# DeltaNet scan with an MLP-mixer on one core: the channel product in 15 block products, joins of units in pairs, a shorter weight rounding, norms on ScalarE, and a new written order

## The chip, the cores and the metric

One core of one Trainium2 chip runs the whole program. The metric is the device time of one launch in microseconds (us). The kernel before was timed three times: 692.44 us median (691.64 to 694.02).

## The reference

There are two stages. The first is a linear-attention scan ("DeltaNet") over 4 elements of 8 heads, 768 tokens and 48 features. For each token `t`, with `k_n = k / (|k| + 1e-6)`:

```
y[t]   = q[t] @ state
v_old  = k_n[t] @ state
state += beta[t] * outer(k_n[t], v[t] - v_old)
```

The second takes `x`, which is `y` as 4 x 768 tokens x 384 channels, and applies two small networks, first over tokens and then over channels:

```
h   = relu(x^T @ w_tok1) @ w_tok2          # 768 -> 256 -> 768 tokens
u   = x + h^T
out = u + relu(u @ w_ch1) @ w_ch2          # 384 -> 1536 -> 384 channels
```

Weights arrive as float64 and are rounded to float32 on the chip.

## The kernel before, in words

**The scan.** Each element's tokens are cut into 6 units of 128 tokens, 24 units in all, and each unit into two steps of 64 tokens, 48 steps. For each unit `prep(u)` (job `p`) squares and sums the keys, forms the norms (L396 to L403), transposes keys and queries on TensorE (L412, L428), multiplies them (L443) and masks the products on VectorE (L450). The masked 64x64 triangles need an inverse. `invert(rnd)` (job `i`) inverts their 32x32 diagonal blocks for a round of up to four units together, in a long series of pairs of VectorE operations (L561, L566). `join(u)` (job `j`) then fills the off-diagonal 32x32 block with two small products: `p_z` (L627), which ScalarE copies to `zst` (L630), and `p_x` (L636), copied into place (L639). Units 0 to 5 are inverted in 16x16 blocks first, with a smaller join, `join_16` (job `h`, L596 to L612), half of whose copies run on VectorE (`EARLY_DVE`). `recur(t)` (job `r`) takes one step of the scan: `p_k` (L660), `rest` on VectorE (L664), `p_y` and `p_w` (L677, L681), a ScalarE copy (L685), `p_s` and `p_y` (L693, L694), the new state on VectorE (L703), and the output rows on ScalarE (L708).

**The weights.** 34 pieces (jobs `w`) come by DMA as 64-bit words. `round_weights` takes each through six operations: on ScalarE a scaling of the low words (L256) and a square of the high words (L268), on GpSimd an add (L269), and on VectorE a shift (L257), an insertion of the sign (L262), and a compare-and-multiply (L271) that sets values of tiny magnitude to zero.

**The mixer.** `mixer(b)` (job `m`) is one element's second stage: the token products (L818, L831), then the channel products for three pairs of 128-token chunks. For element 0 the first channel product is plain: 12 tiles of hidden channels x 3 blocks of 128 input channels over 256 tokens (L904). For elements 1 to 3 `wide_fast` does it with sums of blocks: of the 12 block products that 2 x 3 blocks on 2 chunks need it makes 11, in two groups of three tiles each, so 66 products of 128x128 by 128x128 for each pair (L749). TensorE runs each product as two instructions here, so 132. The results are collected in `r2` by ScalarE copies (L776 to L795), VectorE adds (L766) and ScalarE relus (L769). The sums of weight blocks come from `sum_weights` (job `s`, L727); the sums of token blocks are four VectorE operations in `turn_pair` (L869). The second channel product has seven block products of 12 instructions each (L923) into two accumulators, `p_o` and `p_o2`. VectorE makes the operands `s1`, `s2` and `a21` (`halves_of`, L885) and adds the accumulators to `xb` (L849).

**The order.** Nothing is scheduled automatically. Every job is a generator, and a long string, `order`, lists which job takes its next step. Each engine executes its own instructions in the order in which that string issues them. `x`, `z`, `Y` are products of zeros on TensorE (L205, L215), whose results nobody reads. The last word is `m3*114`: the last 114 steps of element 3's mixer stand alone.

PSUM tiles of the mixer come from a pool of three banks (`ps_mlp`); a bank's next product waits until its last reader is done.

Of the kernel before, what the change touches and what calls it, by code (L numbers as in the profile page):

```python
# [13 lines left out]
C = 64  # L14
# [9 lines left out]
def kernel(  # L24
# [82 lines left out]
    EARLY_DVE = (1, 3)  # L107
# [6 lines left out]
    nc.scalar.sqrt(warm[0:1, 128:129], warm[0:1, 128:129])  # L114
    ident = const.tile([128, 128], FP32, name="ident")
# [65 lines left out]
    wcs = lent[:, 0 : 3 * NM * 128].rearrange("p (i m n) -> p i m n", i=3, m=NM)  # L181
# [60 lines left out]
    def round_weights(dst, src, name):  # L242

        n = dst.shape[-1]
        d64 = loads.tile([128, WP], mybir.dt.int64, name="d64", bufs=3)[:, 0:n]  # L250
        nc.sync.dma_start(out=d64, in_=src)
        yield
        words = d64.bitcast(U32).rearrange("p (n two) -> p n two", two=2)
        lo, hi = words[:, :, 0], words[:, :, 1]
        f = mlp_pool.tile([128, WP], U32, name="w_f", tag="r1")[:, 0:n]
        nc.scalar.activation(lo, lo, ACTF.Copy, scale=2.0**-29)  # L256
# [5 lines left out]
        nc.vector.scalar_tensor_tensor(  # L262
            out=f, in0=hi, scalar=0xC0000000, in1=f,
            op0=ALU.bitwise_and, op1=ALU.bitwise_or,
        )
        yield
        a = hi.bitcast(FP32)
        nc.scalar.square(a, a)  # L268
# [111 lines left out]
    def prep(u):  # L380
# [15 lines left out]
        nc.scalar.sqrt(nrm_f, ksum)  # L396
        yield
        nc.vector.tensor_scalar_add(nrm_f, nrm_f, 1e-6)
        cs = work.tile([128, NP, 2], FP32, name="cs")
        rec = work.tile([128, NB], FP32, name="rec")  # L400
        nc.vector.reciprocal(rec, nrm_f)
        nc.vector.tensor_tensor(out=rec, in0=rec, in1=rec, op=ALU.mult)
        nc.vector.tensor_tensor(  # L403
            out=cs, in0=rec.rearrange("s (p c) -> s p c", c=2), in1=bet, op=ALU.mult
# [180 lines left out]
    def join_16(u):  # L585
# [24 lines left out]
        for i, (block, _, _) in enumerate(quarters(u)):  # L610
            on = nc.vector.tensor_copy if i in EARLY_DVE else nc.scalar.copy
            on(out=block[0:QB, :, QB:HB], in_=p_x[HB * i : HB * i + QB])  # L612
            joined_16.add((u, i))
            yield

    def join(u):
# [3 lines left out]
        halves = [(slice(r.start, r.start + HB), slice(r.start + HB, r.stop)) for r in PAR]  # L620
        assert done.issuperset([(u, 0), (u, 2)])
        nc.vector.transpose(t11, wt[:, :, 0:HB])
        yield
        p_z = ps_prep([128, NB, HB], "p_z")
        for nb in range(NB):
            for r, r2 in halves:
                nc.tensor.matmul(p_z[r2, nb], wt[r, nb, HB:C], t11[r, nb])  # L627
        yield
        for r, r2 in halves:
            nc.scalar.copy(zst[r2], p_z[r2])  # L630
        yield
        assert done.issuperset([(u, 1), (u, 3)])
# [5 lines left out]
        for r, r2 in halves:  # L638
            nc.scalar.copy(wt[r, :, HB:C], p_x[r])  # L639
# [73 lines left out]

    def sum_weights():
        a = wc1.rearrange("p cb (m k n) -> p cb m k n", m=NM, k=2)
        for cb in range(2):
            for f in range(NHT):
                piece_of(wc1, cb, f * 128)
        a11, a21, a12, a22 = a[:, 0, :, 0], a[:, 0, :, 1], a[:, 1, :, 0], a[:, 1, :, 1]
        s1, s2, s4 = (wcs[:, i] for i in range(3))  # L720
        for i, (out, x, y, op) in enumerate((
            (s1, a21, a22, ALU.add), (s2, s1, a11, ALU.subtract),
            (s4, a12, s2, ALU.subtract), (a21, a11, a21, ALU.subtract),
        )):
            if i == 3:
                assert FAST in starts
            nc.vector.tensor_tensor(out=out, in0=x, in1=y, op=op)  # L727
            summed.add(i)
            yield

    starts = set()

    def wide_fast(u_t, t, r2):
        own = u_t[:, :, 0:U], u_t[:, :, U : 2 * U]
        b11, b21, b22 = own[0][:, 0], own[0][:, 1], own[1][:, 1]
        t1, t2, t4, t3 = t[:, 0], t[:, 1], t[:, 2], own[1][:, 0]
        def w(m, cb, k):
            f = (2 * m + k) * 128
            return wc1[:, cb, f : f + 128]

        lo, hi = slice(0, U), slice(U, 2 * U)
        n = NM // 2

        def bank(name):
            return ps_mlp([128, n, U], name)

        def product(p, weight, b_, first=False):
            for i in range(n):
                nc.tensor.matmul(  # L749
                    p[:, i], weight(g * n + i), b_, start=first and i == 0, stop=True,  # L750
                    skip_group_check=True,
                )

        def plain(cb, k):
            return lambda m: w(m, cb, k)

        def mixed(i):
            assert i in summed
            return lambda m: wcs[:, i, m]

        for g in range(2):
            ms = slice(g * n, g * n + n)
            c11, c12, c21, c22 = (r2[:, ms, k, e] for k in range(2) for e in (lo, hi))

            def add(out, p):
                nc.vector.tensor_tensor(out=out, in0=p, in1=out, op=ALU.add)  # L766

            def relu(out):
                nc.scalar.activation(out, out, ACTF.Relu)  # L769

            p_r = bank("p_r")
            product(p_r, plain(1, 0), b21, True)
            yield
            p_x = bank("p_c")
            product(p_x, plain(0, 0), b11, True)
            nc.scalar.copy(c11, p_x)  # L776
            yield
            product(p_r, plain(2, 0), own[0][:, 2])
            add(c11, p_r)
            yield  # L780
            p_y = bank("p_d")
            product(p_y, mixed(0), t1, True)
            nc.scalar.copy(c22, p_y)
            yield
            product(p_x, mixed(1), t2)
            nc.scalar.copy(c12, p_x)
            yield
            p_r = bank("p_r")
            product(p_r, plain(1, 1), t4, True)
            product(p_r, plain(2, 1), own[0][:, 2])  # L790
            relu(c11)
            yield
            assert 3 in summed
            product(p_x, plain(0, 1), t3)
            nc.scalar.copy(c21, p_x)  # L795
            yield
            product(p_y, mixed(2), b22)
            product(p_y, plain(2, 0), own[1][:, 2])
            add(c21, p_r)
            add(c12, p_y)  # L800
            yield
            product(p_x, plain(2, 1), own[1][:, 2])
            relu(c21)
            relu(c12)
            add(c22, p_x)
            yield
            relu(c22)
            yield
            yield g * n + n - 1

    def mixer(b):
# [42 lines left out]
        def turn_pair(c):  # L854
# [6 lines left out]
            t = mlp_pool.tile([128, 3, U], FP32, name="t_c", tag="r1")  # L861
            b11, b21, b12, b22 = (
# [239 lines left out]
```

## Time and profile before

| | |
|---|---|
| Median of three runs | 692.44 us (691.64 to 694.02) |
| The profiled execution's own time | 692.83 us |
| Its span in the profile | 691.0 us |
| Mean granted TensorE clock | 0.936 |
| Read from HBM, written to HBM | 35.49 MB, 9.44 MB |

The span runs from the first to the last instruction of the profiled execution; 1.8 us of its time lie around it. In the profile PE is TensorE's matmuls, PEld its weight loads (which run ahead beside matmuls), DVE is VectorE, ACT ScalarE, POOL GpSimd and SP the queue that issues DMAs. Line numbers are those of the kernel before. In a list of groups the columns are: line, engine, operation, out<-in, shape, xcount | busy us, mean ns of one | idle time ahead, and what ended it. In a timeline they are: start us, length us, engine, line, operation, xcount [idle ahead <- what ended it].

### The profile page before, as it was taken

Reading aid. Unit: us, or ns where it says so; the run is one execution under the profiler, and the core shown is the slowest. Engines: PE = TensorE matmul, PEld = TensorE weight load, DVE = VectorE, ACT = ScalarE, POOL = GpSimd, SP = SyncE. Lnnn points to the kernel's source line nnn. Section 1 sums busy time; section 2 is a strip of 40 time slices with the busy share of each in tenths; the row PEclk is TensorE's granted clock in tenths of the full one; section 3 lists DMA queues with packets and bytes.
Section 4 is the critical chain, followed back from the end, with each engine's and each line's share of the span. In section 5 each row is a group of like instructions: output and inputs, shape, how many; then the busy total and the mean of one; then the engine's idle time right before and its main releaser. Section 6 shows DMA issues by size and latency. Waiting matters only on the chain.

```text
span 691.0 us, 22497 instructions
## 1 busy us (share of the span) xinstructions
PE 643.6 (93%) x9696; PEld 562.2 (81%) x9696; DVE 428.9 (62%) x1135; ACT 272.7 (39%) x659; POOL 103.1 (15%) x121
## 2 busy tenths in 40 slices
PE   7548977689999999999999999999999999999998
PEld 5336766557899998877999999868989996999997
DVE  6988677887888853696464985347823332252433
ACT  7647666334732243213642514234425051132230
POOL 1345245213420112010120100100000000000000
PEclk9757677579999999999999999999999999999999
DMA  9744565545453334322444004020020000000000
GB/s 183 153 102 108 116 147 119 148 119 124 91 107 83 78 67 82 84 49 65 70 75 98 15 24 84 28 54 9 17 63 2 16 10 0 24 1 24 1 24 24
DMA packets 146915, 46.39 MB, mean 67 GB/s; under 512 B 138080, under 2 KB 141280, under 8 KB 146816
## 3 DMA queue, kind: packets, MB, share of 16 engines
q1 hardware_dynamic: 146816, 44.95, 29.8%
q8 instruction: 76, 1.25, 0.8%
q14 instruction: 23, 0.19, 0.1%
HBM read 35.49 MB, written 9.44 MB: 65 GB/s over the span
## 4 chain that ended last, share of the span: by engine, by line
PE 81%; DVE 7%; DMA 3%; SPq 3%; ACT 3%; issue 2%; POOL 0%; DVEq 0%; ACTq 0%; POOLq 0%
PE p_o L923 24%; PE p_r L749 8%; PE p_c L749 7%; PE p_d L749 5%; PE p_c L904 5%; PE p_h L831 5%; PE p L818 4%; PE p_k L660 4%; PE p_y L677 3%; PE p_g L443 3%; PE p_s L693 3%; PE p_z L627 2%; DVE sub L561 2%; PE p_warm L205 2%; PE p_x L636 2%
## 5 line engine op out<-in xcount | busy, mean ns | idle before, releaser
L923 PE MATMUL p_o<-wc,r 128*128 128x192 f32 x720 | 126.4, 329 | 0.6 <-ACT u_t L845 0.6
L923 PEld LDWEIGHTS p_o<-wc,r 128*128 128x128 f32 x720 | 116.6, 190 | 2.4 <-ACT u_t L845 1.1
L849 DVE TENSOR_TENSOR xb<-xb,p_o 128x192 f32<-128x192 f32 x84 | 29.5, 352 | 69.9 <-PE p_o L923 69.4
L561 DVE TENSOR_TENSOR sub<-x 128x84 f32<-128x84 f32 (+24 forms) x178 | 60.4, 339 | 8.1 <-DMA x<-n_dram 4.4
L566 DVE TENSOR_TENSOR x<-x,sub 128x84 f32<-128x84 f32 (+24 forms) x178 | 60.1, 338 | 6.1
L766 DVE TENSOR_TENSOR r<-p_r,r 128x384 f32<-128x384 f32 x36 | 20.0, 555 | 53.5 <-ACT r L795 42.2
L364 POOL TENSOR_TENSOR v_st<-v_st,nrm 128x384 f32<-128x384 f32 x24 | 20.6, 860 | 211.9 <-DMA v_st<-in_v_dram 187.0
L923 PE MATMUL p_o<-wc,s 128*128 128x192 f32 x288 | 50.7, 329 | 0.7 <-DVE xb L849 0.7
L904 PE MATMUL p_c<-u_t,wc 128*128 128x256 f32 x216 | 50.3, 385 | 0.0
L708 ACT ACTIVATE xb<-p_y 64x192 f32<-64x192 f32 x96 | 31.2, 325 | 47.0 <-PE p_y L694 20.4
L269 POOL TENSOR_TENSOR w_f<-w_f,d 128x384 uint32<-128x384 uint32 (+1 forms) x34 | 34.0, 1007 | 98.7 <-DVE w_f L262 49.8
L923 PEld LDWEIGHTS p_o<-wc,s 128*128 128x128 f32 x288 | 46.8, 190 | 1.3 <-DVE xb L849 1.0
L749 PE MATMUL p_r<-u_t,wc 128*128 128x128 f32 x324 | 46.5, 280 | 0.0
L749 PE MATMUL p_c<-u_t,wc 128*128 128x128 f32 x324 | 45.3, 276 | 0.0
L904 PEld LDWEIGHTS p_c<-u_t,wc 128*128 128x128 f32 x216 | 39.9, 190 | 5.6 <-issue 0.2
L769 ACT ACTIVATE r<-r 128x384 f32<-128x384 f32 x72 | 37.5, 523 | 17.2 <-DVE r L766 15.1
L685 ACT COPY w_t<-p_w 128x192 f32<-128x192 f32 x48 | 15.3, 319 | 67.8 <-PE p_w L681 67.3
L749 PEld LDWEIGHTS p_r<-u_t,wc 128*128 128x128 f32 x324 | 41.4, 194 | 0.4
L749 PEld LDWEIGHTS p_c<-u_t,wc 128*128 128x128 f32 x324 | 40.5, 192 | 0.2
L450 DVE TENSOR_TENSOR gm<-p_g,mb 128x512 f32<-128x512 f32 x44 | 28.8, 682 | 15.7 <-PE p_g L443 14.8
L776 ACT COPY r<-p_c 128x384 f32<-128x384 f32 x18 | 8.6, 479 | 73.9 <-PE p_c L749 67.8
L818 PE MATMUL p<-xb,w 128*128 128x384 f32 x96 | 36.4, 529 | 0.0
(170 smaller groups left out, 1284.9 us busy)
## 6 DMA issues: line engine op xcount, KB each, us to landing
d<-in_moe_w_ch_dram SPq DMA_DIRECT2D x24, 384.0 KB, 3.8
v_st<-in_v_dram SPq DMA_DIRECT2D x96, 48.0 KB, 2.7
out_dram<-xb SPq DMA_DIRECT2D x23, 192.0 KB, 1.9
kpad<-in_k_dram SPq DMA_DIRECT2D x18, 192.0 KB, 3.9
qpad<-in_q_dram SPq DMA_DIRECT2D x18, 192.0 KB, 3.6
kst<-in_k_dram SPq DMA_DIRECT2D x64, 48.0 KB, 2.8
n_dram<-gm SPq DMA_DIRECT2D x72, 32.0 KB, 2.5
gm<-w_dram SPq DMA_DIRECT2D x72, 32.0 KB, 2.1
```

Source lines behind the costliest of these rows:

```text
L269: nc.gpsimd.tensor_tensor(out=f, in0=f, in1=lo, op=ALU.add)
L450: nc.vector.tensor_tensor(out=blocks(gm)[:, :, cc, D:GW].rearrange("s p (two n) -> s p two n", two=2), in0=p_g[cc], in1=mb[:, :, cc, None, ...
L561: nc.vector.tensor_tensor(out=tmp, in0=y[:, :, 0:s, s : s + 1].to_broadcast([n, k, s, w]), in1=y[:, :, s : s + 1, s + 1 : m].to_broadcast( ...
L566: nc.vector.tensor_tensor(out=y[:, :, 0:s, s + 1 : m], in0=y[:, :, 0:s, s + 1 : m], in1=tmp, op=ALU.add,)
L708: nc.scalar.mul(y[:, :, D * i : D * i + D], p_y[PAR[1 - i]], 1.0 if c else -1.0)
L749: nc.tensor.matmul(p[:, i], weight(g * n + i), b_, start=first and i == 0, stop=True, skip_group_check=True,)
L769: nc.scalar.activation(out, out, ACTF.Relu)
L818: nc.tensor.matmul(p_1[dh], piece_of(w1, c, 0)[:, dh * 128 : (dh + 1) * 128], xb[:, c], start=(c == 0), stop=(c == NCH - 1),)
L831: nc.tensor.matmul(p_h, piece_of(w2, j, c * 128)[:, c * 128 : (c + 1) * 128], r1[j], start=(j == 0), stop=(j == NDH - 1),)
L849: nc.vector.tensor_tensor(out=xb[:, c, e], in0=xb[:, c, e], in1=p, op=ALU.add)
L904: nc.tensor.matmul(p_c[:, k], piece_of(wc1, cb, f * 128)[:, f * 128 : (f + 1) * 128], u_t[:, cb], start=(cb == 0), stop=(cb == NCB - 1),)
L923: nc.tensor.matmul(p, a[:, m], wc2[:, m, j], start=(start and m == 0), stop=(m == NM - 1), skip_group_check=True,)
```

## The change

1. **First channel product, elements 1 to 3.** The 1536 hidden channels are taken as 3 blocks of four tiles, and the 18 block products (3 x 3 blocks on 2 chunks) are made from 15 products of sums. Each has four matmuls, so 60 for a pair of chunks, 120 instructions. The 15 follow each other in four chains, each of which accumulates in one bank; after each product the bank is read into one block of `r2`, once into two. `sum_weights` grows from 4 operations of 768 elements to 17 of 512 or 256, 10 of them written over blocks of the weights, after the plain product of element 0 has used the block. The sums of token blocks (`forms`) grow from 4 to 11 operations. `halves_of` runs after all 15 products, in two parts, and the second channel product takes its tiles in the order 2 to 5, 0, 1.
2. **Joins.** In rounds from unit 6 on, the `p_x` products of a unit are issued between the `p_z` products of the next unit of its round, one for one; the last unit's follow alone.
3. **Rounding.** The compare-and-multiply that sets tiny values to zero is gone; the high word is scaled by 2^-112 on ScalarE instead of squared, and two VectorE operations do what three did.
4. **Norms.** The added 1e-6 and the square move from VectorE to ScalarE.
5. `EARLY_DVE` is gone: the 12 small copies it put on VectorE run on ScalarE.
6. **A new order** string. It ends in `m3*153`. It calls the products of zeros at other places: 8 instead of 11 of the 512-wide, 3 instead of 7 of the 128-wide, 20 instead of 12 of the small ones.

The core of the diff:

```
-        nc.scalar.activation(lo, lo, ACTF.Copy, scale=2.0**-29)
+        a = hi.bitcast(FP32)
+        nc.scalar.activation(a, a, ACTF.Copy, scale=2.0**-112)
+        nc.scalar.activation(lo, lo, ACTF.Copy, scale=2.0**-29)
+        yield
         nc.vector.tensor_scalar(
-            out=f, in0=hi, scalar1=0x07FFFFFF, scalar2=3,
+            out=f, in0=hi, scalar1=0x0FFFFFFF, scalar2=3,
...
-        nc.vector.scalar_tensor_tensor(
-            out=f, in0=hi, scalar=0xC0000000, in1=f,
...
-        nc.scalar.square(a, a)
         nc.gpsimd.tensor_tensor(out=f, in0=f, in1=lo, op=ALU.add)
         yield
         nc.vector.scalar_tensor_tensor(
-            out=dst, in0=a, scalar=(1.125 * 2.0**-15) ** 2, in1=f.bitcast(FP32),
-            op0=ALU.is_ge, op1=ALU.mult,
+            out=dst.bitcast(U32), in0=hi, scalar=0x80000000, in1=f,
+            op0=ALU.bitwise_and, op1=ALU.bitwise_or,
...
         nc.scalar.sqrt(nrm_f, ksum)
-        nc.vector.tensor_scalar_add(nrm_f, nrm_f, 1e-6)
-        nc.vector.reciprocal(rec, nrm_f)
-        nc.vector.tensor_tensor(out=rec, in0=rec, in1=rec, op=ALU.mult)
+        nc.scalar.activation(nrm_f, nrm_f, ACTF.Identity, bias=eps)
+        nc.scalar.square(ksum, nrm_f)
+        nc.vector.reciprocal(ksum, ksum)
...
         for nb in range(NB):
             for r, r2 in halves:
                 nc.tensor.matmul(p_z[r2, nb], wt[r, nb, HB:C], t11[r, nb])
+                if before:
+                    w = gm_of(before)[:, :, TC]
+                    nc.tensor.matmul(p_x[r, nb], zst[r2, nb], w[r2, nb, HB:C])
...
+        for n, (out, x, y, op) in enumerate((
+            ("u5", b[0, 0], b[2, 1], add), ("u12", b[1, 0], b[2, 0], add),
+            ("u3", b[0, 1], b[1, 1], add), ("u2", "u3", b[0, 0], sub),
+            ("u6", b[0, 1], b[0, 0], sub), ("u13", "u12", b[2, 1], sub),
+            ("u7", b[0, 1], b[2, 1], add), ("u4", b[1, 0], "u2", sub),
+            ("u8", "u13", b[1, 1], sub), ("u10", b[0, 0], b[2, 0], add),
+            ("u15", b[2, 0], b[2, 1], sub),
+        )):
...
+        for chain, n, reads in (
+            (1, 1, ((0, 0, 1, 0),)), (4, 12, ((0, 0, -1, 0),)), (2, 5, ((2, 0, 1, 0),)),
+            (1, 2, ((0, 1, 1, 0),)), (4, 13, ((0, 1, -1, 0),)), (2, 6, ((2, 1, 1, 0),)),
+            (1, 3, ((1, 1, 1, 0),)), (4, 14, ((2, 1, 1, 0),)), (1, 4, ((1, 0, 1, 0),)),
+            (2, 7, ((1, 1, 1, 1),)), (3, 10, ((1, 0, 1, 1), (2, 0, -1, 0))),
+            (2, 8, ((2, 1, -1, 1),)), (4, 15, ((2, 0, 1, 1),)), (3, 11, ((0, 0, 1, 1),)),
+            (2, 9, ((0, 1, 1, 1),)),
+        ):
...
+            for i in range(FT):
+                at = i % width * 128
+                nc.tensor.matmul(
+                    p[:, i], pieces[i // width][:, at : at + 128], f[f"u{n}"],
+                    start=first and i == 0, stop=True, skip_group_check=True,
+                )
+            yield
+            for j, e, sign, last in reads:
+                o = part(j, e)
+                if (j, e) not in begun:
+                    nc.scalar.copy(o, p)
+                    begun.add((j, e))
+                else:
+                    nc.vector.tensor_tensor(
+                        out=o, in0=o, in1=p, op=ALU.add if sign > 0 else ALU.subtract
+                    )
+                if last:
+                    nc.scalar.activation(o, o, ACTF.Relu)
+            yield
+        yield slice(2, NM)
+        yield slice(0, 2)
```

More of the change, by code (lines that the diff above doesn't have):

```diff
@@ L623, in join, with into @@
         yield
+        def into(x, w):
+            for r, r2 in halves:
+                nc.scalar.copy(w[r, :, HB:C], x[r])
+        assert len(left_over) == (not first)
+        before = None if first else left_over.pop()
+        assert first or done.issuperset([(before, 1), (before, 3)])
         p_z = ps_prep([128, NB, HB], "p_z")
+        p_x = ps_prep([128, NB, HB], "p_x") if before else None
         for nb in range(NB):
@@ L630, in join @@
             nc.scalar.copy(zst[r2], p_z[r2])
+        if before:
+            into(p_x, gm_of(before)[:, :, TC])
+            joined.add(before)
+        if not last:
+            left_over.append(u)
         yield
+        if not last:
+            return
         assert done.issuperset([(u, 1), (u, 3)])
@@ L731 @@
[L731 to L772, printed above, removed]
-            yield
[L774 to L809, printed above, removed]
@@ L893, in mixer @@
             if b >= FAST:
[L894 to L896 removed]
+                for ms in wide_fast(t_c, r2):
+                    if ms is not None:
+                        halves_of(ms)
                     yield
```

292 lines of the change are left out of this document (173 added, 119 removed).

## The prediction

> **What bounds the kernel now.** I read the page first, then its stretches, and cut them where step 11 of the scan, element 0's last, begins; from there the mixer can run.
>
> ```profile
> span 691.0 us, 22497 instructions
> PE 643.6 (93%) x9696; PEld 562.2 (81%) x9696; DVE 428.9 (62%) x1135; ACT 272.7 (39%) x659; POOL 103.1 (15%) x121
> PE   7548977689999999999999999999999999999998
> PEclk9757677579999999999999999999999999999999
> ```
> ```profile
> 145.65 0.35 DVE L664 TENSOR_TENSOR rest<-p_k,v_st 128x192 f32<-128x192 f32 x1
> ```
> ```profile
> 0.00:145.65 145.65, 104.89 (x2544) 79.45 (x2545) 115.79 (x326) 86.85 (x212) 50.87 (x66) 0.73 0.62 134
> 145.65:350.00 204.35, 203.16 (x3242) 171.93 (x3241) 144.82 (x385) 80.99 (x203) 37.97 (x40) 0.98 0.39 83
> 350.00:560.00 210.00, 208.54 (x2992) 192.55 (x2991) 120.17 (x320) 72.45 (x177) 14.21 (x16) 0.99 0.18 39
> 560.00:691.00 131.00, 127.02 (x924) 118.22 (x922) 48.10 (x107) 32.43 (x69) 0.00 (x0) 1.00 0.04 13
> ```
>
> The columns after the stretch are its length, then busy us of PE, PEld, DVE, ACT and POOL, clock, DMA share, GB/s. There are two kernels here. Until 145.65 us VectorE is the busiest engine (115.79 of 145.65, 79%), ScalarE has 60%, and TensorE has a granted clock of 0.73. After it PE is full. But weight loads, which cannot overlap their own kind so freely, fill 84%, 92% and 90% of the three later stretches: TensorE sets the pace there, with some 60 us of gaps that the long matmul ends hide. So work taken from TensorE after 145.65 us counts in full, unless a new wait takes its place.
>
> **Part 1: the early stretch (rounding, norms, early copies).**
>
> ```profile
> L262 DVE SCALAR_TENSOR_TENSOR w_f<-d,w_f 128x384 uint32<-128x384 uint32 (+1 forms) x34 | 19.1, 571 | 0.4
> L402 DVE TENSOR_TENSOR rec<-rec 128x8 f32<-128x8 f32 x24 | 4.8, 199 | 0.8
> L398 DVE TENSOR_SCALAR nrm<-nrm 128x8 f32<-128x8 f32 x24 | 4.2, 176 | 0.4 <-ACT nrm L396 0.3
> L612 DVE COPY gm<-p_x 16x128 f32<-16x128 f32 x8 | 2.3, 290 | 2.0 <-ACT gm L612 1.8
> ```
> ```profile
> L256 ACT ACTIVATE d<-d 128x384 uint32<-128x384 uint32 (+1 forms) x34 | 18.2, 539 | 9.3 <-DMA d<-in_moe_w_ch_dram 6.8 <-DMA d<-in_moe_w_tok_dram 2.4
> L268 ACT ACTIVATE d<-d 128x384 f32<-128x384 f32 (+1 forms) x34 | 18.0, 538 | 9.0 <-DVE w_f L262 8.9
> L396 ACT ACTIVATE nrm<-ksum 128x8 f32<-128x8 f32 x24 | 5.0, 207 | 13.0 <-DVE ksum L391 12.9
> L612 ACT COPY gm<-p_x 16x128 f32<-16x128 f32 x8 | 2.0, 253 | 0.4 <-PE p_x L606 0.3
> ```
>
> In both written orders 26 of the 34 weight pieces and 11 norms stand on VectorE ahead of step 11. VectorE loses there 26/34 of 19.1 us = 14.6, 11 x (0.176 + 0.199) = 4.1, and 12 copies x 0.29 = 3.5: 22.2 us. ScalarE gains 22 small operations x 0.207 = 4.6 and 12 copies x 0.253 = 3.0: 7.6 us. Its two rounding operations stay two; the one that waited for VectorE (8.9 us of idle behind L262) now starts with the DMA. The shift now waits for that operation, 0.54 us later for each piece; pieces are loaded well ahead, so I cost it at nothing, and at 26 x 0.54 = 14 us if no piece were.
>
> The gain of time is between 22 us (VectorE alone sets the end) and nothing (transfers and the step-by-step chain do); below nothing if ScalarE, at (86.85 + 7.6) / 145.65 = 65%, became the last, at most 7.6 us. Between them the chain of waits inside this stretch decides:
>
> ```profile
> by line: issue 9.2%; DVE sub L561 6.6%; PE p_warm L205 6.5%; DVE x L566 5.5%; SPq L355 4.6%; PE p_g L443 3.9%; DMA x<-n_dram 3.9%; DVE w_f L262 3.7%; PE p_k L660 3.5%; PE p_z L596 3.2%; DMA kpad<-in_k_dram 3.1%; DMA lent<-in_k_dram 2.8%; DV
> ```
>
> VectorE stands in it, but among all the others. I take half, 11 us, and 1 us for three fewer of the 512-wide products of zeros: **-12 us**. The new order's moves of loads in the SP queue are inside that range.
>
> **Part 2: the joins.** The 13 units from 6 on that have a follower in their round get their `p_x` issued between another unit's `p_z`, so that four 32x32 places of the array are in use and not two.
>
> ```profile
> 61.59 0.63 PEld L596 LDWEIGHTS p_z<-r,gm 32*32 32x32 f32 x64 [0.55 <-DVE gm L450]
> 62.19 0.58 PEld L627 LDWEIGHTS p_z<-t,wc 32*32 32x32 f32 x32
> 62.81 0.31 PEld L660 LDWEIGHTS p_k<-s_t,wc 48*64 48x64 f32 x8
> ```
>
> 64 instructions on four places start 62.19 - 61.59 = 0.60 us before the next group; 32 on two places take 62.81 - 62.19 = 0.62. A merged 64 should take about 0.6 us where two groups took 1.24, which is 13 x 0.62 = 8 us at best. But L596 has half as many moving columns, and the merged group waits for both units' copies. I take 0.5 us each: **-6.5 us**, with 0 and -8 as ends.
>
> The Trainium skill ("TensorE: Matmul & The Clock Gate", section "Wait — 56ns, not 53.3ns?") speaks against this: starts of matmuls never come closer than about 25 ns, however small they are. By it 64 instructions would take 1.6 us, merged or not, and this term would be 0 and the time 682.3 us. The rows disagree: 64 in 0.60 us is 9 ns each.
>
> **Part 3: the channel product, what it saves.**
>
> ```profile
> 630.20 0.75 PEld L749 LDWEIGHTS p_r<-u_t,wc 128*128 128x128 f32 x6
> 630.87 0.75 PEld L749 LDWEIGHTS p_d<-t_c,lent 128*128 128x128 f32 x6
> ```
>
> Six instructions take 0.67 us, so 0.1117 each. 132 - 120 = 12 fewer in each of 9 pairs: 108 x 0.1117 = **-12.1 us**. One of the 15 products is 8 instructions, 0.89 us.
>
> **Part 4: what the channel product adds in waits.** Element 3 runs alone at the end, and there the new order can be walked through.
>
> ```profile
> 631.25 0.56 DVE L766 TENSOR_TENSOR r<-p_r,r 128x384 f32<-128x384 f32 x1 [1.72 <-PE p_r L749]
> 639.22 0.55 DVE L766 TENSOR_TENSOR r<-p_r,r 128x384 f32<-128x384 f32 x1
> 639.83 0.74 PEld L749 LDWEIGHTS p_r<-t_c,wc 128*128 128x128 f32 x6 [0.17 <-DVE r L766]
> 645.74 0.74 PEld L841 LDWEIGHTS p_ut<-ident,xb 128*128 128x128 f32 x6
> 647.01 1.11 PEld L923 LDWEIGHTS p_o<-wc,r 128*128 128x128 f32 x7 [0.54 <-ACT u_t L845]
> 619.06 3.93 PEld L923 LDWEIGHTS p_o<-wc,s 128*128 128x128 f32 x24
> 622.96 5.88 PEld L923 LDWEIGHTS p_o<-wc,r 128*128 128x128 f32 x36
> ```
> ```profile
> L450 DVE TENSOR_TENSOR gm<-p_g,mb 128x512 f32<-128x512 f32 x44 | 28.8, 682 | 15.7 <-PE p_g L443 14.8 <-POOL mb L421 0.7 <-issue 0.2
> L885 DVE TENSOR_TENSOR s<-r 128x384 f32<-128x384 f32 x24 | 13.8, 573 | 9.6 <-ACT r L769 6.2 <-ACT r L911 3.3
> L727 DVE TENSOR_TENSOR wc<-wc 128x768 f32<-128x768 f32 x1 | 0.9, 950 | 0.0
> L869 DVE TENSOR_TENSOR t_c<-u_t 128x128 f32<-128x128 f32 x9 | 2.6, 288 | 3.0 <-ACT u_t L845 3.0
> L849 DVE TENSOR_TENSOR xb<-xb,p_o 128x192 f32<-128x192 f32 x84 | 29.5, 352 | 69.9 <-PE p_o L923 69.4
> L911 ACT ACTIVATE r<-p_c 128x512 f32<-128x512 f32 x18 | 10.8, 598 | 31.3 <-PE p_c L904 31.3
> ```
>
> A product's reader starts 631.25 - 630.20 = 1.05 us after its first load with six instructions, so 1.27 with eight. A VectorE read of 512 takes 0.68 (L450), a ScalarE copy 0.60 (L911), and a load follows the read by 0.06 (639.22 + 0.55 to 639.83): the bank is free again 2.01 or 1.93 us after the first load. Two products later is 1.79. In the list's order a bank comes again after two products three times: 7th to 9th (chain 1), the 9th's bank handed to chain 3's first, the 11th, and 10th to 12th (chain 2). That is 0.14 + 0.14 + 0.22 = 0.5 us.
>
> Then VectorE's queue, from the first load of the 15th product: its read ends at 1.95. `halves_of`, formerly half done by now, is three operations of 512 (0.70, between L885 and L727) and three of 256 (0.43): 5.34. The add of `p_o` (L849): 5.69. 11 sums of tokens x 0.29, formerly four: 8.9. The add of `p_o2`: 9.25. TensorE: product 15 to 0.89, the first of the second channel product (12 loads in 1.95 us, a half of 619.06 to 622.96) to 2.84, turning 1.27 (645.74 to 647.01) to 4.11, the second to 6.06, the third to 8.01. The fourth starts `p_o2` afresh and waits until 9.25 + 0.06: 1.3 us. In the last pair of an element there is nothing to turn; there the third waits for the add of `p_o`, 5.75 against 4.79: 0.96 us.
>
> So a pair alone waits 1.8, 1.8 and 1.45 us; before it waited 0.17. Each of element 3's pairs saves 1.34 and pays 1.63 or 1.28: nothing is left there. It pays 4.6 us. In elements 1 and 2 the order puts scan steps and joins between those products in most pairs; I charge a little over half, 0.9 us x 6 = 5.4. **+10 us**, with +5 (all covered there) and +15 (none) as ends.
>
> **Part 5: VectorE in the middle.** Per pair its reads and sums were 8 x 0.56 + 4 x 0.29 = 5.6 us and become 10 x 0.68 + 11 x 0.29 = 10.0. Six pairs: +26. Weight sums: 15 x 0.70 + 2 x 0.43 - 4.3 = +7. Remaining rounding and norms: -9. So 24 us more on 265 of 414 us, 64% to 70%. Scan steps wait on VectorE, and TensorE's queue waits for them in order. This costs between 0 and 24 us; where VectorE is busier (71% in 145 to 350 against 57% in 350 to 560) weight loads fill 84% against 92%, so some of it does come out. **+4 us**, nearer to nothing, since TensorE has other jobs in its queue.
>
> **Sum.** -12 - 6.5 - 12.1 + 10 + 4 = -16.6. The profiled execution took 692.83 us, its span 691.0 with 1.8 around it: 676.2. The median of the runs is 0.4 lower: 675.8, say **676 us**.
>
> **Rivals.**
> 1. *The early stretch does not shorten*: its end is set by transfers and the chain of steps, and VectorE only idles more. For it: transfers share 62% and the mixed chain. Against it: VectorE at 79%. Part 1 is 0: 688 us.
> 2. *VectorE's queue becomes the bound of elements 1 and 2* (slower): every wait of part 4 uncovered (+15) and every added microsecond of part 5 on the path (+24), for -12 - 6.5 - 12.1 + 39 = +8: 701 us. It turns slower once parts 4 and 5 together pass 31 us. For it: the waits worked out above. Against it: VectorE stays at 70%.
> 3. *All gains come through*: part 1 in full (-22), joins -8, waits only in element 3 (+5), part 5 nothing: -37, 655 us.
> 4. *It does not do what it says*: the moved work gives back what it saves everywhere and the time stays within 0.3% of 692.4.
>
> **How the numbers follow.** Forecast (667 to 684) 0.50; rival 1 0.18; rival 3 0.16; rival 4 0.06; rival 2 0.10. About 0.3% is what a measurement here can tell from no change. Faster: 0.50 + 0.18 + 0.16 = 0.84; same 0.06; slower 0.10. The range runs from 655 (rival 3) to 693 (rival 4 in it), and leaves out rival 2 and the far side of rival 3.
>
> **What would show it.** Part 1: step 11's `rest` near 134 us and not 145. Part 2: 64 loads of `p_z` and `p_x` in about 0.7 us. Part 3: 0.1117 us per load in the 15 products. Part 4: in element 3 a wait of 1.3 us on an add of `p_o2`, and pairs still near 30 us. Part 5: loads at 84% or more from there to element 3. Wrong it would be if the granted clock of the early stretch fell well below 0.73, or if the products of zeros at their new places delayed the scan.

## The result, and the profile after

The changed kernel takes **668.57 us** (median of four runs, 666.09 to 674.38), the kernel before 692.04 in the same job (690.87 to 694.02). The ratio is 0.967, with a 95% interval of 0.960 to 0.974. Two more series of the same kernel, run beside the experiments, gave 0.9698 and 0.9688. That is 23.5 us less (21 to 22 by the two later series) where 16.6 were forecast: direction right, inside the range, the gain a quarter to two fifths larger than the sum. The profiled execution took 667.63 us, its span is 665.8. Some executions of a kernel take over 1.5% longer than its fastest; the ratios leave these out, and of two profiled executions that are such (in the second of the two later series, and in the run with VectorE's early work put back) the time ahead of step 11 counts in no mean or difference below.

The page of the changed kernel, with the lines that answer those of before:

```profile
span 665.8 us, 22344 instructions
PE 620.0 (93%) x9590; PEld 541.9 (81%) x9590; DVE 440.9 (66%) x1136; ACT 278.9 (42%) x683; POOL 103.4 (16%) x121
PE   5558886898999998999999999999999999999998
PEclk9958678699999999999999999999999999999999
```

TensorE has 106 instructions fewer (108 fewer in the channel product, two more of zeros) and 20.3 us less of weight loads. VectorE has 12 us more. Step 11 of the scan, which the prediction used as the cut, and the stretches on both sides of it (length, then busy us of PE, PEld, DVE, ACT and POOL, clock, DMA share, GB/s):

```profile
138.43 0.35 DVE L683 TENSOR_TENSOR rest<-p_k,v_st 128x192 f32<-128x192 f32 x1
```
```profile
0.00:138.43 138.43, 101.40 (x2554) 79.77 (x2554) 103.05 (x270) 93.17 (x248) 49.94 (x65) 0.79 0.67 139
138.43:350.00 211.57, 206.73 (x3438) 175.67 (x3437) 152.06 (x393) 89.53 (x230) 43.28 (x45) 0.99 0.41 85
350.00:560.00 210.00, 210.00 (x2881) 187.62 (x2880) 131.99 (x350) 71.69 (x165) 10.20 (x11) 1.00 0.16 35
560.00:665.80 105.80, 101.92 (x725) 98.90 (x723) 53.84 (x127) 24.47 (x42) 0.00 (x0) 1.00 0.05 16
```

Step 11 comes 7.2 us earlier (145.65 to 138.43), and from there to the end it is 527.4 us where it was 545.4: 18.0 less. Where in that second part, the first load of each mixer's token product shows, elements 1, 2 and 3, before and then after:

```profile
302.46 0.35 PEld L818 LDWEIGHTS p<-xb,w 128*128 128x128 f32 x2
446.74 0.62 PEld L818 LDWEIGHTS p<-xb,w 128*128 128x128 f32 x3
568.22 0.94 PEld L818 LDWEIGHTS p<-xb,w 128*128 128x128 f32 x4
```
```profile
294.01 3.58 PEld L868 LDWEIGHTS p<-xb,w 128*128 128x128 f32 x12
432.24 0.94 PEld L868 LDWEIGHTS p<-xb,w 128*128 128x128 f32 x4
547.38 0.62 PEld L868 LDWEIGHTS p<-xb,w 128*128 128x128 f32 x3
```

The lead is 8.45 us at element 1, 14.5 at element 2, 20.8 at element 3 and 25.2 at the end. So the mixers give 6.1, 6.3 and 4.4 us. The prediction had expected no gain in element 3. There 2.1 of the 4.4 lie ahead of the turn of tokens to its second pair, where the written order still mixes in the end of element 2; behind it only the channel product differs.

How steady are these two parts? The code up to step 11 is the same in eight profiled executions (three of the changed kernel, five of experiments that differ only later). In seven of them step 11 begins between 136.1 and 142.7 us, 139.5 on average; the eighth is the long one of the second series (145.9). The rest is steadier: 527.4, 529.3 and 528.6 us in the three executions of the changed kernel, mean 528.4, that is **17.0 us less** than before; 525.7 in the last experiment below, whose code behind step 11 is the same. The kernel before has one profiled execution only. The gains by ratio, 21 to 23 us in all, leave 4 to 6 for the early part. So that part is read as **about 5 us less**, with some 3 us of scatter to either side in any one execution, and the later part to about 2 us.

The early scatter goes with TensorE's granted clock. Ahead of step 11 it is 0.81 and 0.82 in the executions that reach step 11 at 136.1 and 139.0 us, 0.77 and 0.75 in those at 141.6 and 142.7, and 0.73 in the kernel before at 145.65. Which of the two brings the other about isn't shown.

### The profile page after: what moved, and what is told of

Read it like the earlier page. It is cut to its first block, busy times and chain, and to the rows that moved or that the text cites. A ratio compares the mean times of both kernels' runs of the same rounds, so it can differ in the third digit from the quotient of the medians.

```text
span 665.8 us, 22344 instructions
## 1 busy us (share of the span) xinstructions
PE 620.0 (93%) x9590; PEld 541.9 (81%) x9590; DVE 440.9 (66%) x1136; ACT 278.9 (42%) x683; POOL 103.4 (16%) x121
## 4 chain that ended last, share of the span: by engine, by line
PE 78%; DVE 6%; SPq 2%; DMA 2%; issue 2%; ACT 1%; POOL 0%; DVEq 0%; ACTq 0%; POOLq 0%
PE p_o L970 25%; PE p_r L840 19%; PE p_c L948 6%; PE p_h L881 4%; PE p L868 4%; PE p_k L679 3%; PE p_s L712 3%; PE p_g L441 3%; PE p_y L696 3%; DVE x L564 1%; PE p_z L637 1%; DVE sub L559 1%; PE p_t L426 1%; DMA d<-in_moe_w_ch_dram 1%; PE p_w L700 1%
## 5 line engine op out<-in xcount | busy, mean ns | idle before, releaser
L852 DVE TENSOR_TENSOR r<-r,p_r 128x512 f32<-128x512 f32 x90 | 60.3, 684 | 40.6 <-PE p_r L840 40.3
L849 ACT COPY r<-p_r 128x512 f32<-128x512 f32 x54 | 31.5, 586 | 82.3 <-PE p_r L840 69.2
L559 DVE TENSOR_TENSOR sub<-x 128x84 f32<-128x84 f32 (+24 forms) x178 | 59.0, 332 | 5.5 <-DMA x<-n_dram 1.6
L948 PEld LDWEIGHTS p_c<-u_t,wc 128*128 128x128 f32 x216 | 40.6, 194 | 7.2 <-ACT u_t L895 1.7
L856 ACT ACTIVATE r<-r 128x512 f32<-128x512 f32 x54 | 33.8, 630 | 25.3 <-DVE r L852 24.9
L419 POOL TENSOR_TENSOR mb<-mask_c,cs 128x512 f32<-128x512 f32 x20 | 21.4, 1071 | 116.1 <-DVE cs L401 115.7
L840 PE MATMUL p_r<-u_t,wc 128*128 128x128 f32 x288 | 38.3, 276 | 0.0
L840 PE MATMUL p_r<-t_d,wc 128*128 128x128 f32 x288 | 37.8, 280 | 0.0
L840 PEld LDWEIGHTS p_r<-u_t,wc 128*128 128x128 f32 x288 | 35.4, 192 | 0.2
L441 PE MATMUL p_g<-kqt 64*64 64x128 f32 x704 | 29.1, 300 | 6.8 <-ACT kqt L430 6.8
```

Source lines behind the costliest of these rows:

```text
L441: nc.tensor.matmul(p_g[cc][PAR[i ^ cc], p], kqt[PAR[i], 2 * p + cc, 0], kqt[PAR[i], 2 * p + cc],)
L559: nc.vector.tensor_tensor(out=tmp, in0=y[:, :, 0:s, s : s + 1].to_broadcast([n, k, s, w]), in1=y[:, :, s : s + 1, s + 1 : m].to_broadcast( ...
L840: nc.tensor.matmul(p[:, i], pieces[i // width][:, at : at + 128], f[f"u{n}"], start=first and i == 0, stop=True, skip_group_check=True,)
L849: nc.scalar.copy(o, p)
L852: nc.vector.tensor_tensor(out=o, in0=o, in1=p, op=ALU.add if sign > 0 else ALU.subtract)
L856: nc.scalar.activation(o, o, ACTF.Relu)
```

## The experiments

Each experiment's time is compared with the changed kernel by the ratios to the kernel before on the same chip; the changed kernel's mean of the two series below is 0.9693, and 0.01 is 6.9 us.

### The changed kernel again

> The changed kernel once more, beside the others of its call, as the point from which they are measured. Both theories: 668 to 670 us, a ratio of about 0.967 to the kernel before.

> The changed kernel again, as the point from which the others of this call are measured: 668 to 672 us, a ratio of 0.966 to 0.973 to the kernel before.

Measured: 670.5 us, 0.9698 (0.9663 to 0.9732), and 669.95 us, 0.9688 (0.9648 to 0.9729). The result stands.

### Joins one behind the other

```
         for nb in range(NB):
             for r, r2 in halves:
                 nc.tensor.matmul(p_z[r2, nb], wt[r, nb, HB:C], t11[r, nb])
-                if before:
-                    w = gm_of(before)[:, :, TC]
-                    nc.tensor.matmul(p_x[r, nb], zst[r2, nb], w[r2, nb, HB:C])
+        for nb in range(NB if before else 0):
+            for r, r2 in halves:
+                w = gm_of(before)[:, :, TC]
+                nc.tensor.matmul(p_x[r, nb], zst[r2, nb], w[r2, nb, HB:C])
```

> The changed kernel, but a unit's 16 p_x products are issued behind the 16 p_z products of the next unit and not between them; same steps, same order, same results. Theory (four places of the array work side by side, and TensorE sets the pace after step 11): each of the 13 pairs of groups takes 1.1 to 1.2 us and not 0.6, and the kernel gets 5 to 8 us slower, 674 to 677. Rival (instructions of this size are limited by their number, or the time is hidden by gaps of TensorE): 0 to 1 us, 668 to 670.

> The kernel of e1 again, beside the changed kernel on one chip. In the profile of e1 the 13 pairs of groups took 1.04 us and not 0.70, together 4.4 us. Theory (TensorE's time counts after step 11): from step 11 to the end 3 to 6 us longer than the changed kernel, and the time 2 to 6 us longer. Rival (gaps take it in): both within 1.5 us.

Measured: 670.78 us, 0.9709 (0.967 to 0.9748), and 672.95 us, 0.9725 (0.9683 to 0.9767): 1.1 and 2.2 us more, with intervals that overlap those of the changed kernel. The times alone don't tell the theory from the rival. The trace sees more, as the part after step 11 is steadier: 533.1 and 531.7 us (step 11 at 139.02 and 141.64) against 528.4, 4.0 more on average. That is within the second forecast (3 to 6) and below the first (5 to 8). One merged group of the changed kernel, its first and last loads and the first load of the next group:

```profile
237.54 0.10 PEld L637 LDWEIGHTS p_z<-t,gm 32*32 32x32 f32 x1
...
238.08 0.10 PEld L640 LDWEIGHTS p_x<-gm,zst 32*32 32x32 f32 x1
238.22 0.30 PEld L970 LDWEIGHTS p_o<-wc,r 128*128 128x128 f32 x2
```

Such a pair of groups in the experiment, where the two follow each other:

```profile
354.55 0.52 PEld L637 LDWEIGHTS p_z<-t,gm 32*32 32x32 f32 x28
...
355.03 0.52 PEld L641 LDWEIGHTS p_x<-gm,zst 32*32 32x32 f32 x27
355.59 1.92 PEld L971 LDWEIGHTS p_o<-wc,r 128*128 128x128 f32 x12
```

64 loads take 238.22 - 237.54 = 0.68 us when they alternate, 355.59 - 354.55 = 1.04 when they follow each other; the 13 merged groups have a mean of 0.71. 13 x 0.33 = 4.3 us, and 4.0 came out. In the kernel before, a group that stands alone takes 0.62, so two take 1.24. But behind step 11 ten of its 36 groups already stood side by side, in five pairs, and four of these pairs took 1.04. One of them:

```profile
175.94 0.52 PEld L636 LDWEIGHTS p_x<-gm,zst 32*32 32x32 f32 x28
...
176.97 0.13 PEld L677 LDWEIGHTS p_y<-s_t,kqt 48*64 48x64 f32 x1
```

(The fifth took 2.54, with 1.41 of idle time in it whose cause the profile doesn't name.) So standing side by side is new for 8 of the 13 and worth another 8 x 0.21 = 1.7.

### VectorE's early work put back

```
+        nc.vector.scalar_tensor_tensor(
+            out=f, in0=hi, scalar=0x80000000, in1=f,
+            op0=ALU.bitwise_and, op1=ALU.bitwise_or,
+        )
...
-        nc.scalar.activation(nrm_f, nrm_f, ACTF.Identity, bias=eps)
-        nc.scalar.square(ksum, nrm_f)
+        nc.vector.tensor_scalar_add(nrm_f, nrm_f, 1e-6)
+        rec = work.tile([128, NB], FP32, name="rec")
+        nc.vector.reciprocal(rec, nrm_f)
+        nc.vector.tensor_tensor(out=rec, in0=rec, in1=rec, op=ALU.mult)
...
-            nc.scalar.copy(block[0:QB, :, QB:HB], p_x[HB * i : HB * i + QB])
+            on = nc.vector.tensor_copy if i in (1, 3) else nc.scalar.copy
+            on(out=block[0:QB, :, QB:HB], in_=p_x[HB * i : HB * i + QB])
```

The new order stays; the third rounding operation, the norms and half of the small copies go back to VectorE.

> The changed kernel with its order, but VectorE gets its early work back: the sign of each weight piece is inserted twice (a third VectorE operation, same result), the norms' add and square are on VectorE, and so are the 12 small copies. Ahead of step 11 that is 22 us more VectorE work. Theory (VectorE's relief brought step 11 forward by 7 us): step 11's rest near 145 us and the time 5 to 9 us longer, 674 to 678. Rival (the new order brought it forward): step 11 stays near 138 and the time within 2 us of 668.6.

Measured: 685.48 us, 0.988 (0.9829 to 0.9931): 12.9 us more by the ratios, and more than the theory gave. Its part after step 11 is 532.2 us in the one execution that was profiled, 3.8 more than the changed kernel's. What is left, some 9 us and uncertain by 4, lies ahead of step 11. So in the new order VectorE's early work counts.

### The relief alone, in the old order

The kernel before, with the new rounding, the norms on ScalarE and all small copies on ScalarE (the edits of parts 3, 4 and 5 of the change, and no other).

> The kernel before with its own order, and of the change only the shorter rounding, the norms on ScalarE and the 12 copies on ScalarE. Theory (VectorE's relief brings step 11 forward): step 11's rest near 138 us and not 145.65, and the time 5 to 8 us shorter than before, 684 to 687. Rival (the order did it): within 2 us of before, 690 to 694.

Measured: 694.3 us, 1.0046 (1.0019 to 1.0073): 3 us **slower** than before. The theory fell here, and the time lies just past the rival's range too. Stretches of 20 us over the first 160, the kernel before and then the experiment:

```profile
sum 160.00, PE 118.74 PEld 87.43 DVE 126.21 ACT 91.04 POOL 55.56; mean PE 14.84 PEld 10.93 DVE 15.78 ACT 11.38 POOL 6.95
```
```profile
sum 160.00, PE 118.47 PEld 88.00 DVE 107.84 ACT 97.83 POOL 52.46; mean PE 14.81 PEld 11.00 DVE 13.48 ACT 12.23 POOL 6.56
```

VectorE does 18.4 us less, as intended, and TensorE still does the same work in that time: VectorE only idles. Step 11 even begins later in the profiled execution, and VectorE's longest new wait (engine, line, what it waits for, us in all, times, longest) is the one that the prediction had cost at nothing, the shift behind ScalarE's scaling:

```profile
151.05 0.35 DVE L660 TENSOR_TENSOR rest<-p_k,v_st 128x192 f32<-128x192 f32 x1
```
```profile
DVE w_f L262 <- ACT d L259: 13.1, 9, 3.0
```

From step 11 on it is 693.0 - 151.05 = 542.0 us, 3.4 less than before, so the loss lies ahead of it.

### The old order, rounding without that wait

```
         nc.vector.scalar_tensor_tensor(
             out=f, in0=hi, scalar=0xC0000000, in1=f,
             op0=ALU.bitwise_and, op1=ALU.bitwise_or,
         )
         yield
-        a = hi.bitcast(FP32)
-        nc.scalar.square(a, a)
-        nc.gpsimd.tensor_tensor(out=f, in0=f, in1=lo, op=ALU.add)
+        nc.gpsimd.tensor_tensor(out=dst.bitcast(U32), in0=f, in1=lo, op=ALU.add)
         yield
-        nc.vector.scalar_tensor_tensor(
-            out=dst, in0=a, scalar=(1.125 * 2.0**-15) ** 2, in1=f.bitcast(FP32),
-            op0=ALU.is_ge, op1=ALU.mult,
-        )
```

The kernel before with two VectorE operations for each piece of weights instead of three, one ScalarE operation instead of two, and no wait of VectorE for ScalarE. Norms and copies stay on VectorE.

> The kernel before with its own order, and only the compare-and-multiply of the rounding and the square that feeds it left out (values under 2^-126 are not set to zero): GpSimd's add writes the weights. VectorE has one operation fewer for each piece, ScalarE one fewer, and the shift waits for the DMA alone, as before. Theory (in e4 the shift's new wait for ScalarE ate the relief): step 11 at 135 to 142 us, 682 to 688. Rival (with the old order VectorE's relief does not move step 11 at all): within 2 us of before, 690 to 694.

Measured: 689.41 us beside 689.9, 0.9985 (0.9953 to 1.0016): no gain. VectorE's work is not relieved as far as in the run above, as norms and copies stay. Step 11 begins 1.8 us earlier, which is within its scatter:

```profile
143.84 0.35 DVE L658 TENSOR_TENSOR rest<-p_k,v_st 128x192 f32<-128x192 f32 x1
```

So the wait for ScalarE isn't the whole reason why the relief alone brings nothing: without that wait the old order doesn't use it either. The rival held.

### The changed kernel with that rounding

The same rounding put into the changed kernel, which takes one ScalarE operation for each piece away and leaves VectorE's two.

> The changed kernel with its own order, and the rounding of e10 in place of its own: the same two VectorE operations for each piece, but no scaling of the high word on ScalarE and no wait of the shift for it (values under 2^-126 are not set to zero). ScalarE loses 26 x 0.53 = 14 us ahead of step 11. Theory (the shift's wait and ScalarE's load still cost time in the changed kernel): 2 to 8 us shorter, 662 to 668. Rival (its order has covered that wait): within 2 us of 670.

Measured: 673.78 us, 0.9742 (0.9701 to 0.9784): not shorter, by 3.4 us the other way with intervals that overlap. The theory fell. Taking ScalarE's 34 added operations away in this manner, which also lets VectorE insert the sign one step earlier and GpSimd write the weights last, wins nothing back.

### TensorE's saved work put back

```
+            for i in range(3 if n in (12, 13) else 0):
+                nc.tensor.matmul(
+                    p[:, i], pieces[0][:, i * 128 : (i + 1) * 128], f[f"u{n}"],
+                    start=False, stop=True, skip_group_check=True,
+                )
```

Six more matmuls for each pair of chunks, twelve instructions, as many as before; their results are added in and make the output another than the reference's.

> The changed kernel with 12 more TensorE instructions in each of the 9 pairs: products 2 and 5 of the 15 repeat six of their matmuls into the same bank, so the output is not the reference's. TensorE's count in the first channel product is then that of the kernel before, 132. Theory (after step 11 TensorE sets the pace and its work counts in full): 108 x 0.1117 = 12 us longer, 681 to 684. Rival (TensorE's gaps there take it in, the gain came from the order): 0 to 5 us, 670 to 675.

Measured: 680.28 us, 0.9844 (0.9803 to 0.9886): 10.4 us more, and 539.0 after step 11 (at 136.08) against 528.4, **10.6 more** of 12.1 at most. The rival, 0 to 5, fell. In element 3 a pair takes 630.80 - 600.82 = 29.98 us (the first product after the turn of tokens, to the same of the next pair):

```profile
600.82 1.92 PEld L975 LDWEIGHTS p_o<-wc,r 128*128 128x128 f32 x12 [0.53 <-ACT u_t L900]
630.80 1.92 PEld L975 LDWEIGHTS p_o<-wc,r 128*128 128x128 f32 x12 [0.54 <-ACT u_t L900]
```

### The sums of token blocks twice

```
+            nc.vector.tensor_tensor(out=spare_f, in0=x, in1=y, op=op)
```

Behind each of the 11 sums, into a tile that nobody reads.

> The changed kernel with each of the 11 sums of token blocks made twice, the second time into a tile that nobody reads; same results. VectorE's queue ahead of the add of p_o2 grows by 11 x 0.2 = 2.2 us. Theory (in element 3 that queue ends just as the next product is due, a margin near 0): each of element 3's first two pairs waits 2 us more, and of the six in elements 1 and 2 half or less: 4 to 10 us longer, 674 to 680. Rival (VectorE has slack there, which is why the predicted wait did not show): within 2 us of 670.

Measured: 688.13 us, 0.9959 (0.9932 to 0.9985): 18.4 us more, far over what theory or rival gave. The timeline of element 3, the first sum and its double, and then the wait of the fourth product:

```profile
609.36 0.28 DVE L811 TENSOR_TENSOR t_d<-u_t 128x128 f32<-128x128 f32 x1
609.56 0.28 DVE L812 TENSOR_TENSOR spare_c<-u_t 128x128 f32<-128x128 f32 x1
...
614.18 0.35 DVE L902 TENSOR_TENSOR xb<-xb,p_o 128x192 f32<-128x192 f32 x1
614.58 1.92 PEld L973 LDWEIGHTS p_o<-wc,s 128*128 128x128 f32 x12 [2.48 <-DVE xb L902]
```

The operations start 0.20 us apart, so 9 x 11 of them are 20 us of VectorE, and nearly all of it comes out. Elements 1 and 2 pay it as well: from one mixer's first token product to the next, and from the last one to the end, it is 145.5, 120.7 and 124.9 us, against 138.2, 115.2 and 118.4 in the changed kernel. That is rival 2's mechanism: it is real, and it begins right behind the place where the changed kernel stands.

### Fewer sums of token blocks

Five of the 11 sums are left out, and plain blocks or another sum stand in for them, so the output is not the reference's; TensorE's work stays.

```
-            "u12": t6[:, 2], "u13": t6[:, 3], "u8": t6[:, 4], "u10": t6[:, 5],
+            "u12": t6[:, 2], "u13": t6[:, 2], "u8": b[1, 1], "u10": b[0, 0],
...
+            if n not in (5, 6, 8, 9, 10):
+                nc.vector.tensor_tensor(out=f[out], in0=x, in1=y, op=op)
```

> The changed kernel with 5 of the 11 sums of token blocks left out (other blocks stand in their place, so the output is not the reference's). VectorE's queue ahead of the add of p_o2 is 5 x 0.2 = 1 us shorter for each pair, 9 us in all. Theory (the written order leaves that queue a margin near 0, so that more work comes out in full but less brings little): 0 to 3 us shorter, 667 to 671. Rival (VectorE is the bound of elements 1 and 2 also in the changed kernel): 5 to 9 us shorter, 661 to 665.

Measured: 671.07 us, 0.9709 (0.968 to 0.9738), and 527.1 us after step 11: 1.3 less there, nothing in the whole. The rival, 5 to 9 us shorter, fell: more sums come out nearly in full, fewer bring nothing.

### No products of zeros

`keep_warm` and `warm_tiles` keep their places in the order and issue nothing.

> The changed kernel without any of the products of zeros; same results. Theory (they only fill TensorE's idle time and hold its granted clock up in the early stretch): the clock ahead of step 11 falls from 0.79 to 0.7 or less, and step 11 comes 0 to 6 us later, 670 to 676. Rival (they stand in the way, as the chain of waits before had them with 6.5% of that stretch): step 11 comes 3 to 8 us earlier, 662 to 667.

Measured: 671.7 us, 0.9719 (0.9687 to 0.9751), 1.8 us more with intervals that meet. Stretch of the first 140 us, after and then the experiment:

```profile
0.00:140.00 140.00, 102.49 (x2588) 80.52 (x2588) 104.59 (x272) 93.82 (x250) 51.46 (x67) 0.79 0.67 139
```
```profile
0.00:140.00 140.00, 95.88 (x2397) 80.05 (x2397) 96.74 (x255) 89.11 (x237) 49.61 (x64) 0.65 0.64 133
```

Without them the granted clock of the early stretch falls from 0.79 to 0.65. Step 11 begins at 145.9 us, later than in any of the seven executions above (136.1 to 142.7), but the part behind it is 525.7 us, the shortest of all with this code. So in the whole these products bring about 2 us or nothing; whether they bring step 11 forward by more, the one execution doesn't settle.

## Why the prediction was right, and where not

**Part 1, the early stretch (forecast -12, measured about -5).** ScalarE's busy time up to step 11 rose from 86.85 to 93.17 us, 6.3 where the working had 7.6. VectorE's fell from 115.79 to 103.05, only 12.7 where the working had 22.2 from durations; the same relief in the old order took 18.4 off the first 160 us. Step 11 came at 138 to 140 and not near 134; the sign of a fallen clock did not show (0.79 after 0.73). The size and the reason failed. The prediction took half of VectorE's relief as gain, on the ground that VectorE stands among the links of the chain. Relief alone brings nothing (0.9985) or a loss (1.0046); with the new order, taking the relief away costs some 9 us ahead of step 11, more than the 5 that the change gained there. So neither is a gain by itself, and the two together are. The reading that fits is that an engine that is early in a written order waits for its next line, and that only an order written for the new durations uses the time; which lines do it was not tested, and how much of the 5 us goes with the higher clock isn't known. "I cost it at nothing" for the shift's wait failed too: 13.1 us in nine waits in the old order, and still 6.7 us in six in the new one:

```profile
DVE w_f L263 <- ACT d L260: 6.7, 6, 3.0
```

**Part 2, the joins (forecast -6.5, measured about -6).** The row that it was read from held: 64 on four places in 0.60 us there, a mean of 0.71 here, 11 ns each. The working took two groups apart, 1.24 us, as the state before for all 13; for five it was 1.04. Of the 6 us the alternation, 4.3 by rows, was tested by undoing it (4.0 in the trace; the timed medians alone could not show it); the other 1.7 rest on rows only.

**Part 3, the saved products (forecast -12.1, measured 10.4 to 10.6).** Right in mechanism, and most of the size came out. In element 3 the twelve instructions that were put back cost 29.98 less the 28.65 below, 1.33 us for a pair, against 1.34 in the working.

**Part 4, the new waits (forecast +10): the term that was mis-sized.** The walk through element 3 named the right wait and got its length wrong. Rows from the timeline of element 3 in the changed kernel, from the last products of a pair on; others between them are left out:

```profile
614.09 0.97 PEld L840 LDWEIGHTS p_r<-u_t,wc 128*128 128x128 f32 x8
615.04 2.03 PEld L840 LDWEIGHTS p_r<-t_d,wc 128*128 128x128 f32 x16
616.99 0.97 PEld L840 LDWEIGHTS p_r<-u_t,wc 128*128 128x128 f32 x8
618.78 0.97 PEld L840 LDWEIGHTS p_r<-u_t,wc 128*128 128x128 f32 x8
619.67 1.93 PEld L970 LDWEIGHTS p_o<-wc,r 128*128 128x128 f32 x12
620.59 0.68 DVE L922 TENSOR_TENSOR s<-r 128x512 f32<-128x512 f32 x1
623.72 0.35 DVE L899 TENSOR_TENSOR xb<-xb,p_o 128x192 f32<-128x192 f32 x1
624.74 4.04 PEld L970 LDWEIGHTS p_o<-wc,s 128*128 128x128 f32 x24
625.12 0.28 DVE L809 TENSOR_TENSOR t_d<-t_d,u_t 128x128 f32<-128x128 f32 x1
625.32 0.28 DVE L809 TENSOR_TENSOR u_t<-u_t 128x128 f32<-128x128 f32 x1
626.45 0.35 DVE L899 TENSOR_TENSOR xb<-xb,p_o 128x192 f32<-128x192 f32 x1
```

The prediction laid VectorE's operations end to end by their mean durations. They overlap: a sum lasts 0.28 us, and the next begins 0.20 after it (625.12 to 625.32). The 11 sums took 623.98 to 626.45, 2.5 us and not 3.2, and `halves_of` 620.59 to 623.72, 3.1 and not 3.4. So the add of `p_o2` ended 8.02 us after the first load of product 15 (618.78) where the walk had 9.25. The third and fourth products together took 4.04 us where 24 loads took 3.93 before: a wait of 0.11 us in place of 1.3. In the last pair the wait was 0.57, not 0.96:

```profile
652.76 2.41 PEld L970 LDWEIGHTS p_o<-wc,s 128*128 128x128 f32 x15 [0.57 <-DVE xb L899]
```

The waits for banks, 0.5 us in the walk, came to some 0.28. At two of the three places a product follows 0.95 us behind the last where 0.89 is the usual (as 614.09 to 615.04); at the third, two products take 1.95 and not 1.79 (615.04 to 616.99). They cost a pair next to nothing, as the kernel before had waits of that size too: its 132 loads took 15.03 us (628.81 to 643.84) and the 120 take 13.71 (605.96 to 619.67), 1.32 less where 12 loads are 1.34.

The period, from one pair to the next, says the same. After, the first product behind the turn, pair by pair, and then the same of before:

```profile
594.20 1.92 PEld L970 LDWEIGHTS p_o<-wc,r 128*128 128x128 f32 x12 [0.53 <-ACT u_t L895]
622.85 1.92 PEld L970 LDWEIGHTS p_o<-wc,r 128*128 128x128 f32 x12 [0.53 <-ACT u_t L895]
```
```profile
617.16 1.92 PEld L923 LDWEIGHTS p_o<-wc,r 128*128 128x128 f32 x12 [0.54 <-ACT u_t L845]
647.01 1.92 PEld L923 LDWEIGHTS p_o<-wc,r 128*128 128x128 f32 x12 [0.54 <-ACT u_t L845]
```

28.65 us against 29.85. A pair gains 1.20 of the 1.34 that it saves and pays 0.14, not 1.63. The trace of before already held the overlap, in this row of its timeline:

```profile
619.69 1.02 DVE L885 TENSOR_TENSOR r<-r,s 128x384 f32<-128x384 f32 x2
```

Two operations of a mean of 0.573 us span 1.02, so the second begins 0.45 after the first. The spacing was there to be read, and the duration of one was taken instead. The Trainium skill has it too (Perfetto Trace Analysis, "Optimizing Scalar/DVE Operations"): a profiled latency holds the write acknowledgement, which "overlaps with the next instruction". The trace agrees that the end of an operation overlaps, here 0.08 us of 0.28; what that end holds no run shows.

**Part 5, VectorE in the middle (forecast +4).** Only its sum with part 4 can be read. After step 11 the time fell by 17.0, known to about 2; the joins give 6.0 and the products 10.6, so parts 4 and 5 together cost nothing that can be told where the forecast had 14. The relief of the later rounding and norms is contained in this, 3.8 by its being put back and 3.4 by its being done alone, one execution each; without it parts 4 and 5 would be some 3 us. How these split between the two stays open. The sign for part 5, loads at 84% or more, missed by little: they fill 83% and 89% of the two middle stretches, after 84% and 92%. What "TensorE has other jobs in its queue" was meant to cover wasn't slack: doubling the sums costs 18.4 us. The sums as they are just fit: leaving five out gained nothing.

**The rivals.** Rival 1 (no gain early) is off by about 5 us, though its reason, that VectorE only idles more, is what the relief alone does. Rival 2 (VectorE's queue, 701) did not occur; doubling the sums brings its mechanism about, at 18.4 us where the rival had 39. Rival 3 (655) was right that waits hardly come, and wrong on the early stretch. Forecast against measured: early -12 and about -5, later -4.6 and -17.0. The two errors partly cancel, so that 676 came as close as it did is in part luck.

**What stays open.** Which pieces of the new order bring step 11 forward was not tried one by one, nor the old order with the new channel product; so a gain of the new order itself behind step 11 can't be excluded within the 2 us. Neither the changed rounding nor fewer sums gave a version that is faster than the changed kernel.

## What to carry to other kernels

For a walk through an engine's queue take the distance between starts of like operations in the trace, not the duration of one: here 0.20 against 0.28 us, and with 11 operations a pair that decided whether TensorE waited. Where the queues are written out by hand, don't price the relief of a busy engine by its share of busy time: here it was worth nothing in the order written for the old durations. Time the relief in the old order and the new order without it before either is credited. Doubling an added cost tells how much room is left behind it; here it was next to none.

## What the runs showed of the hardware

- VectorE operations of 128x128 last 0.28 us and start 0.20 apart, or 0.32 where one reads what the one just before wrote, or writes over what that one read (624.38 to 624.71, 625.93 to 626.24 in the changed kernel). Of 128x256 they last 0.42, and the next starts 0.34 behind, or 0.45 where it reads what the one before wrote:

```profile
622.59 0.42 DVE L922 TENSOR_TENSOR s<-r 128x256 f32<-128x256 f32 x1
623.04 0.42 DVE L922 TENSOR_TENSOR s<-s,r 128x256 f32<-128x256 f32 x1
623.38 0.42 DVE L922 TENSOR_TENSOR r<-r 128x256 f32<-128x256 f32 x1
```

- 64 weight loads of 32x32 take 0.68 us on four alternating places (11 ns each), 1.04 in two groups behind each other, and 2 x 0.62 in groups that stand apart.
- With the products of zeros left out the granted clock ahead of 140 us fell from 0.79 to 0.65, and the time changed by about 2 us, within its noise.
- The same early code reached step 11 between 136.1 and 142.7 us in seven executions, at granted clocks of 0.81 and 0.75, while the part behind it repeated within 4 us (525.7 to 529.3).
